# Sixteen rows of one K tile in each layer are loaded apart, in loads of eight partitions

## The chip, the cores and the metric

The kernel runs on one core of one Trainium2 chip. The metric is the device time of one execution in microseconds; several executions are timed and the median is taken. One more execution is recorded by the hardware profiler, and all rows shown come from that one.

## The reference, cut to what matters

Two layers of attention over a cache and a gated mixer, for a batch of 2 and one new token, all in bfloat16:

```python
def _A_ref(x, k_cache, v_cache, wq, wo):      # k_cache, v_cache: (2, 32, 16384, 128)
    q = (x @ wq).reshape(B, Sq, H, Dh).transpose(0, 2, 1, 3)
    scores = einsum("bhqd,bhkd->bhqk", q, k_cache) * (Dh ** -0.5)
    p = softmax(scores)
    o = einsum("bhqk,bhkd->bhqd", p, v_cache)
    return o.transpose(0, 2, 1, 3).reshape(B, Sq, H * Dh) @ wo

x = x + _A_ref(_layernorm(x), k_cache, v_cache, wq, wo)     # layer 0
x = x + _B_ref(_layernorm(x), w1, w2, w3, w4)               # a small mixer
x = x + _A_ref(_layernorm(x), k_cache, v_cache, wq, wo)     # layer 1
x = x + _B_ref(_layernorm(x), w1, w2, w3, w4)
```

Each layer reads the whole cache: 64 heads (batch times 32) with 4 MB of K and 4 MB of V each. With two layers less one pair that is kept, and the weights, 1092 MB are read.

## The kernel before

Heads are handled in pairs, 32 pairs a layer. A pair's K, and its V, is one tile of 8 MB: 128 partitions, 65536 bytes in each. Partition p holds 256 consecutive tokens of one head (64 partitions a head), so a tile is 128 rows that lie in memory one after the other.

On-chip memory has three slots for tiles. In the steady part of a layer slot A takes each pair's K and slot V each pair's V; the third is work space. `Store` (line 269) keeps a queue of planned loads (`plan`, line 278), each with a name, a semaphore, a place, a size and a list of transfers. A load is issued as soon as the cells of its place are free (`pump`, line 289), by SyncE (SP) through `Graph.dma` (line 85), which issues the listed transfers one after the other on one semaphore; its full count is 16 for each transfer, and who needs the tile waits for the full count. All data loads go through SP's one queue, in the planned order K(s), V(s-1), K(s+1), V(s) and so on (`tile_order`, line 639).

When a K tile has landed, GpSimd (POOL) passes this on to TensorE and VectorE (`landed`, line 1319; the relay is line 187 of the profile). VectorE multiplies half of the tile's blocks by q (`product`, line 1489) and sums later (`gather`, line 1501). TensorE transposes the other half (`transposed`, line 1405), ScalarE copies the transposed blocks out (`evacuate`, line 1428), and TensorE makes the scores (`scores`, line 1438). When the last block of the K tile has been read, SP issues the next K into slot A. Then comes the softmax of this pair and, when its V has landed, p times V of the pair before (`pv`, line 1567), after which SP issues the next V. Pairs 2 to 30 of layer 0 and 3 to 30 of layer 1 run in a loop.

`plan_tile` (line 488) plans a tile's load as one transfer of 128 partitions, or in column parts where `cuts` are given. `plan_all` (line 549) calls it for every tile of layer 0 (line 569) and, for layer 1, in a loop at line 593. `plan_small` (line 541) loads w2 (layer 0) and w1 (layer 1) in two transfers; the second has the last 64 rows of the weight and goes to partitions 64 to 127 alone. In layer 0 it stands in the queue right ahead of the first K tile.

Of the kernel before, what the change touches and what calls it, by code (L numbers as in the profile page):

```python
# [338 lines left out]
class KB:  # L339
# [28 lines left out]
    }  # L368
    PART = 46592
    REST = [(55808, 9728), (46592, 9216)]  # L370
    LAST_V = [(0, 32768), (32768, 16384), (49152, 16384)]
    EC = 96

# [111 lines left out]
    def slot(self, i):  # L485
        return self.AUX + self.EXTRA + i * self.TILE

    def plan_tile(self, T, t, u, slot, cuts=None):
        b, j = u % self.B, u // self.B
        src = T[b, 2 * j:2 * j + 2].rearrange("h (p j) d -> (h p) (j d)", p=self.HALF)  # L490
        if cuts is None:
            self.store.plan((t, u), f"tile{slot}", self.slot(slot), self.TILE, [(lambda m: m, src)])
            return
        have = self.parts.get((t, u), (0, []))[1]
        self.parts[t, u] = self.slot(slot), have + [lo for lo, n in cuts] + [0] * ((t, u) == self.partly())
        for lo, n in cuts:
            self.store.plan((t, u, lo), f"part{slot}_{lo // 4096}", self.slot(slot) + lo, n,
                            [(lambda m: m, src[:, lo // 2:(lo + n) // 2])])
# [50 lines left out]
    def plan_all(self):  # L549

        B, D = self.B, self.D
        row, w3r, wqr = 2 * D, 2 * self.F, 2 * 128 * self.H
        g = [row * n + CELL for n in self.GROUPS[1]]
        self.cuts, self.korder = {}, {}
        s = [self.slot(i) for i in range(self.NSLOT)]
        source = {"k": self.K, "v": self.V}

        tiles = self.tile_order(0)
        V, A, C = range(3)
        assert tiles[:2] == [("k", 0), ("k", 1)]  # L560
        assert tiles[-3:] == [("k", self.W - 1), ("v", self.W - 2), ("v", self.W - 1)]
        full = lambda k, m, at: (k, 0, m, at)
        hd, mt = self.H, self.MT
        self.store.plan(None, "xin", 0, 0, [(self.rows[0:B, :], self.A_x.rearrange("b s d -> (b s) d"))], ["prod"])
        self.plan_cols("wq", 0, self.wq, [full(k, hd, s[C] + wqr * k) for k in range(self.KT)])
        self.plan_small("w2", 0, self.w2, s[C] + wqr * (self.KT - 1) + wqr // 2, (0, 64))
        for i, (t, u) in enumerate(tiles):
            last = i == len(tiles) - 1
            self.plan_tile(source[t], t, u, C if i == 1 or last else A if t == "k" else V, self.LAST_V if last else None)
        r8 = row * self.HG  # L570
        assert r8 == w3r

        def halves(n, pieces):
            return [(k, (h or 0) * n // 2, n if h != 0 else n // 2, at) for k, h, at in pieces]
        w = self.WINDOW
        self.plan_heads(0, w["wo"], 2)
        self.plan_cols("w3", 0, self.w3, halves(mt, w["w3"]))
        self.plan_groups(0, w["w4"])
        self.plan_cols("wq", 1, self.wq, halves(hd, w["wq"]))

        tiles = self.tile_order(1)
        assert tiles[:2] == [("k", self.W - 2), ("k", 0)] and tiles[2] == self.partly()
        tiles[:3] = tiles[2], tiles[0], tiles[1]
        q = self.TILE // 4
        e = self.HOLD * self.CH * 256
        two = [(2 * q * j, 2 * q) for j in range(2)]
        self.plan_tile(source["k"], *tiles[1], A, [(0, e)])
        self.plan_tile(source["v"], *tiles[0], V, self.REST)
        self.plan_tile(source["k"], *tiles[1], A, [(e, q - e)] + [(q * j, q) for j in range(1, 4)])
        self.plan_tile(source["k"], *tiles[2], C, two)  # L590
        assert tiles[4][0] == "v" and tiles[5][0] == "k"
        for i, (t, u) in enumerate(tiles[3:]):
            self.plan_tile(source[t], t, u, C if i == len(tiles) - 4 else A if t == "k" else V, two if i in (1, 2) else None)
        assert t == "v"
        a = s[V]
        ats = []
        for _, lo, hi in self.cuts["wo", 0][-2:]:
            ats.append(row * (hi - lo))
        ats = [r8] * (self.ng - 1) + ats
        ats = [a + sum(ats[:i]) for i in range(len(ats))]  # L600
        self.plan_heads(1, ats)
        a += r8 * self.ng
        self.plan_small("w1", 1, self.w1, a, (0, 64))
        a += row * self.KT
        self.plan_cols("w3", 1, self.w3, [full(k, mt, a + w3r * k) for k in range(self.KT)])
        a += w3r * (self.KT - 1) + w3r // 2
        assert a % CELL == 0 and a + sum(g) <= self.size
        self.plan_groups(1, [a + sum(g[:i]) for i in range(len(g))], CELL)
# [1056 lines left out]
```

## Time and profile before

| | |
|---|---|
| median of 3 runs | 2545.57 us (2545.31 to 2546.1) |
| the profiled execution | 2544.21 us |
| its span on the core | 2542.5 us |
| busy: PE, VectorE, ScalarE, POOL | 56%, 70%, 44%, 1% |
| bytes read | 1092.44 MB, 430 GB/s over the span |
| loads of whole tiles, K and V | 60 and 60 |

The span is the time from the first to the last instruction of the core; the execution's own time is 1.7 us longer. The page gives the busy share of each engine in 40 slices of the span and, beside it, the mean busy share of the core's 16 DMA engines and the rate in GB/s. A table of stretches gives the same for any stretch; it books a DMA packet whole in the stretch in which it starts, so in short stretches the share can exceed 1, while GB/s divided by share remains the rate of those packets. The chain of waits goes back from the last instruction to whatever released it, step by step; a DMA in it is shown from its issue to its landing.

### The profile page before, as it was taken

To read this page: it belongs to the slowest core of one execution; us is meant where nothing else is said; L and a number is where in the kernel's file an instruction comes from. 1 tells how busy PE (TensorE), PEld (TensorE's weight loads), DVE (VectorE), ACT (ScalarE), POOL (GpSimd) and SP (SyncE) were. 2 spreads that over 40 slices of the span, in tenths; PEclk is the share of its full clock that TensorE was granted. 3 is DMA by queue.
4 is the path that set the end of the run, shared out by engine and by line. 5 is a ranking of instruction groups with operands and counts; after the bars stand their busy time and mean duration, and the time that the engine had idled before them with its cause. 6 is when DMAs were issued, how large, how long until landed. Compare 5 with 4: busy or idle time off the path is not lost.

```text
span 2542.5 us, 74290 instructions
## 1 busy us (share of the span) xinstructions
PE 1426.6 (56%) x34671; PEld 1332.8 (52%) x34671; DVE 1767.6 (70%) x1129; ACT 1126.3 (44%) x1705; POOL 29.7 (1%) x100
## 2 busy tenths in 40 slices
PE   4654654654555555546678555555465465555555
PEld 3554544554545545445567555454454455455555
DVE  4876866867767767668439777686686676776773
ACT  3453443543544534534447345345354354453451
POOL 0000000000000000000000000000000000000000
PEclk9665665666656656656656566566566666665665
DMA  9999999999999999999999999999999999999999
GB/s 415 429 434 434 434 432 435 431 434 434 435 434 429 434 435 434 431 437 433 403 411 428 436 430 436 433 434 433 433 435 431 433 434 436 432 433 435 432 431 376
DMA packets 28806, 1093.33 MB, mean 430 GB/s; under 512 B 3146, under 2 KB 4812, under 8 KB 9420
## 3 DMA queue, kind: packets, MB, share of 16 engines
q1 hardware_dynamic: 28748, 1092.45, 99.7%
q8 instruction: 49, 0.80, 0.1%
q14 instruction: 9, 0.07, 0.0%
HBM read 1092.44 MB, written 0.00 MB: 430 GB/s over the span
## 4 chain that ended last, share of the span: by engine, by line
DMA 70%; ACT 13%; PE 12%; issue 2%; DVE 2%; SPq 1%; POOLq 0%; DVEq 0%; POOL 0%
DMA mem<-in_A_v_cache_dram 35%; DMA mem<-in_A_k_cache_dram 33%; ACT mem L1430 12%; PE mps L1576 9%; PE tps L1412 2%; DMA mem<-in_B_w_dram 1%; SPq L98 1%; PE sps L1450 1%; DVE s_dve L1486 1%; DMA mem<-in_A_wo_dram 1%; ACT mem L766 0%; DVE s_dve L1507 0%; DVE prod L1482 0%; DMA mem<-in_A_wq_dram 0%; DVE mem L1497 0%
## 5 line engine op out<-in xcount | busy, mean ns | idle before, releaser
L1430 ACT ACTIVATE mem<-tps 128x1024 bf16<-128x1024 bf16 x835 | 811.4, 1093 | 535.7 <-PE tps L1412 532.5
L1507 DVE TENSOR_REDUCE s_dve<-mem 128x32 f32<-128x4096 bf16 x228 | 1007.1, 4417 | 3.9
L1412 PE MATMUL tps<-ident,mem 128*128 128x128 bf16 x6776 | 600.6, 250 | 718.1 <-POOLq L187 718.1
L1497 DVE TENSOR_TENSOR mem<-mem 128x4096 bf16<-128x4096 bf16 x228 | 507.2, 2287 | 590.9 <-POOLq L187 590.9
L1412 PEld LDWEIGHTS tps<-ident,mem 128*128 128x128 bf16 x6776 | 490.1, 114 | 723.7 <-POOLq L187 723.4
L1576 PE MATMUL mps<-p,mem 128*128 128x2 bf16 x16384 | 450.2, 165 | 94.5 <-POOLq L187 66.6
L1576 PEld LDWEIGHTS mps<-p,mem 128*128 128x128 bf16 x16384 | 443.6, 104 | 106.5 <-POOLq L187 71.7
L1450 PE MATMUL sps<-q_col,mem 128*128 128x2 bf16 x8176 | 360.4, 165 | 156.4 <-ACT mem L1430 133.3
L1450 PEld LDWEIGHTS sps<-q_col,mem 128*128 128x128 bf16 x8176 | 300.9, 98 | 222.1 <-ACT mem L1430 215.6
L1541 ACT ACTIVATE mx<-mx 128x2 f32<-128x2 f32 x64 | 13.0, 203 | 592.0 <-POOL mx L1532 591.9
L1430 ACT ACTIVATE mem<-sps 128x1024 bf16<-128x1024 bf16 x171 | 191.1, 1117 | 0.0
L1412 PE MATMUL sps<-ident,mem 128*128 128x128 bf16 x1464 | 131.9, 243 | 0.4 <-DVE prod L1074 0.4
L1412 PEld LDWEIGHTS sps<-ident,mem 128*128 128x128 bf16 x1464 | 105.1, 111 | 0.5 <-DVE prod L1074 0.5
L1486 DVE TENSOR_REDUCE s_dve<-prod 128x16 f32<-128x2048 bf16 (+1 forms) x44 | 98.5, 2238 | 1.8 <-ACT p L1545 0.4
L1365 ACT ACTIVATE mem<-sps 128x128 bf16<-128x128 f32 x63 | 17.5, 278 | 176.0 <-PE sps L1361 176.0
L1482 DVE TENSOR_TENSOR prod<-mem 128x2048 bf16<-128x2048 bf16 (+1 forms) x44 | 52.8, 1201 | 40.7 <-POOLq L187 39.1
L1361 PE MATMUL sps<-ident,q_col 128*64 128x128 bf16 x126 | 20.0, 314 | 103.0 <-DVE q_col L1348 103.0
L1361 PEld LDWEIGHTS sps<-ident,q_col 128*64 128x64 bf16 x126 | 8.3, 128 | 108.3 <-DVE q_col L1348 108.3
L1545 ACT ACTIVATE p<-s_dve,mx 64x128 bf16<-64x128 f32 (+2 forms) x126 | 54.6, 434 | 13.3 <-PE sps L1558 5.3
L1532 POOL PARTITION_ALL_REDUCE mx<-mx x64 | 25.1, 392 | 2455.4 <-DVE mx L664 2455.4
L1551 ACT ACTIVATE p<-sps,mx 64x128 bf16<-64x128 f32 (+2 forms) x128 | 51.4, 402 | 2.3
L1564 DVE COPY o_acc<-mps 128x2 f32 (+1 forms) x64 | 10.2, 160 | 41.4 <-PE mps L1576 39.5
(119 smaller groups left out, 359.3 us busy)
## 6 DMA issues: line engine op xcount, KB each, us to landing
mem<-in_A_k_cache_dram SPq DMA_DIRECT2D x4, 4096.0 KB, 16.2
mem<-in_A_v_cache_dram SPq DMA_DIRECT2D x3, 4096.0 KB, 21.4
mem<-in_A_wq_dram SPq DMA_DIRECT2D x8, 1024.0 KB, 7.8
mem<-in_B_w_dram SPq DMA_DIRECT2D x14, 576.0 KB, 7.0
mem<-in_A_k_cache_dram SPq DMA_DIRECT2D x3, 2048.0 KB, 12.1
mem<-in_B_w_dram SPq DMA_DIRECT2D x7, 864.0 KB, 21.6
mem<-in_B_w_dram SPq DMA_DIRECT2D x4, 1152.0 KB, 19.2
mem<-in_A_v_cache_dram SPq DMA_DIRECT2D x2, 2048.0 KB, 48.0
```

The lines of the kernel that those rows point to most:

```text
L98: sp.dma_start(dst, src).then_inc(h, 16)
L1361: ins = pe.matmul(qps[e * h:(e + 1) * h, :], lhsT=q, rhs=self.ident[:, :], start=True, stop=True, skip_group_check=True)
L1412: ins = pe.transpose(out[:, j * 128:(j + 1) * 128], buf[:, j * 128:(j + 1) * 128], self.ident[:, :])
L1430: self.act(lambda e: e.activation(out=self.kt[k], in_=src.rearrange("p (i c) -> p i c", i=self.CH), func=ACT.Copy), reads=bk, writes=self. ...
L1450: ins = pe.matmul(self.sps[sp][:, b:b + 2], lhsT=kt[:, j, :], rhs=self.q_col[:, 2 * sp:2 * sp + 2], start=True, stop=True, skip_group_chec ...
L1482: self.dv(lambda e: e.tensor_tensor(out=prod, in0=buf.rearrange("p (j d) -> p j d", d=128), in1=qbc, op=ALU.mult), reads=self.spilt(("qb", ...
L1486: self.dv(lambda e: e.tensor_reduce(out=sd[:, c0:c0 + DB], in_=prod, axis=AX.X, op=ALU.add), reads=["prod"], writes=self.spilt(("s_dve", m ...
L1497: self.dv(lambda e: e.tensor_tensor(out=prod, in0=buf.rearrange("p (j d) -> p j d", d=128), in1=qbc, op=ALU.mult), reads=self.spilt(("qb", ...
L1507: self.dv(lambda e: e.tensor_reduce(out=sd[:, c0:c0 + n], in_=prod, axis=AX.X, op=ALU.add), reads=pk, writes=self.spilt(("s_dve", m)), to= ...
L1545: self.act(lambda e, i=i, at=at: e.activation(out=two(self.p[at, :, i])[:, :, pb:], in_=two(self.s_dve[m][at, 0:self.NB - n]), func=ACT.Ex ...
L1551: self.act(lambda e, i=i, at=at: e.activation(out=two(self.p[at, :, i])[:, :, 0:pb], in_=two(self.sps[m][at, i:2 * n:2]), func=ACT.Exp, bi ...
L1576: ins = pe.matmul(self.mps[:, 448:450], lhsT=buf[:, j * 128:(j + 1) * 128], rhs=self.p[:, b0 + j, :], start=b0 + j == 0, stop=b0 + j == se ...
```

## The change

For two tiles, K of pair 16 in layer 0 and K of pair 16 in layer 1, `plan_tile` lists several transfers in place of one. `UNEVEN` gives for each a number of bytes `at`, 18432 and 0. Partitions 0 to 111 are loaded whole in one transfer. Of partitions 112 to 127, the first `at` bytes of each row are loaded in one transfer of 16 partitions (left out where `at` is 0), and the rest in two transfers, of partitions 112 to 119 and 120 to 127. So layer 0's tile has four transfers and layer 1's three. The bytes, their places, the semaphore of the slot and all instructions of the other engines stay the same; the count that is waited for grows with the number of transfers. The tiles with `cuts` are not touched.

```diff
+    UNEVEN = {(0, "k", 16): 18432, (1, "k", 16): 0}
...
-    def plan_tile(self, T, t, u, slot, cuts=None):
+    def uneven(self, src, at):
+
+        n, a = self.TILE // 2, at // 2
+        rows = [(0, 112, 0, n)] + [(112, 128, 0, a)] * (a > 0) + [(112, 120, a, n), (120, 128, a, n)]
+        return [(lambda m, p=p, q=q, x=x, y=y: m[p:q, x:y], src[p:q, x:y]) for p, q, x, y in rows]
+
+    def plan_tile(self, T, t, u, slot, cuts=None, l=None):
         b, j = u % self.B, u // self.B
         src = T[b, 2 * j:2 * j + 2].rearrange("h (p j) d -> (h p) (j d)", p=self.HALF)
         if cuts is None:
-            self.store.plan((t, u), f"tile{slot}", self.slot(slot), self.TILE, [(lambda m: m, src)])
+            at = self.UNEVEN.get((l, t, u))
+            all_ = [(lambda m: m, src)] if at is None else self.uneven(src, at)
+            self.store.plan((t, u), f"tile{slot}", self.slot(slot), self.TILE, all_)
             return
...
-            self.plan_tile(source[t], t, u, C if i == 1 or last else A if t == "k" else V, self.LAST_V if last else None)
+            self.plan_tile(source[t], t, u, C if i == 1 or last else A if t == "k" else V, self.LAST_V if last else None, 0)
...
-            self.plan_tile(source[t], t, u, C if i == len(tiles) - 4 else A if t == "k" else V, two if i in (1, 2) else None)
+            self.plan_tile(source[t], t, u, C if i == len(tiles) - 4 else A if t == "k" else V, two if i in (1, 2) else None, 1)
```

## The prediction

> **What bounds the kernel now.** I read the slices and the queues on the page first, then the chain of waits, then a table of stretches at the places where the DMA engines differ from each other.
>
> ```profile
> span 2542.5 us, 74290 instructions
> PE 1426.6 (56%) x34671; PEld 1332.8 (52%) x34671; DVE 1767.6 (70%) x1129; ACT 1126.3 (44%) x1705; POOL 29.7 (1%) x100
> ...
> DMA  9999999999999999999999999999999999999999
> GB/s 415 429 434 434 434 432 435 431 434 434 435 434 429 434 435 434 431 437 433 403 411 428 436 430 436 433 434 433 433 435 431 433 434 436 432 433 435 432 431 376
> ...
> q1 hardware_dynamic: 28748, 1092.45, 99.7%
> q8 instruction: 49, 0.80, 0.1%
> ...
> DMA 70%; ACT 13%; PE 12%; issue 2%; DVE 2%; SPq 1%; POOLq 0%; DVEq 0%; POOL 0%
> ```
>
> No compute engine is above 70%, and the data queue's packets fill 99.7% of sixteen engines' span. In the steady slices the rate is 434 GB/s, 27.1 GB/s an engine. A K or V tile is 128 rows of 65536 bytes, eight rows an engine, so one row costs 65536 / 27.1 GB/s = 2.42 us and a tile 19.35 us. A pair (K and V) should take 38.7 us, and the chain at the place of the change shows just that:
>
> ```profile
> 612.87 25.99 DMA mem<-in_A_k_cache_dram
> 638.87 0.02 issue
> ...
> 638.96 1.05 PE tps L1412 x8
> 640.01 0.02 issue
> 640.03 11.11 ACT mem L1430 x12
> 651.14 0.05 issue
> 651.19 0.37 PE sps L1450 x8
> 651.56 0.02 issue
> 651.57 26.00 DMA mem<-in_A_k_cache_dram
> ```
>
> One K is issued at 612.87 and the next at 651.57, 38.70 us later. The next K is issued 12.7 us after the K before it has landed on its last engine (638.87). So every microsecond by which the slowest engine delivers a K later delays the next issue, and as the engines are full, nothing later gives it back.
>
> The engines are not level. The last loads' engines run dry in this table (columns: stretch, its length, busy time and count of PE, weight loads, DVE, ACT and POOL, clock, DMA share, GB/s):
>
> ```profile
> 2534.50:2535.00 0.50, 0.32 (x12) 0.23 (x9) 0.00 (x0) 0.00 (x0) 0.00 (x0) 0.50 0.93 369
> 2535.00:2535.50 0.50, 0.38 (x10) 0.37 (x11) 0.00 (x0) 0.00 (x0) 0.00 (x0) 0.50 0.70 281
> 2535.50:2536.00 0.50, 0.50 (x19) 0.49 (x19) 0.05 (x1) 0.25 (x2) 0.00 (x0) 0.50 0.53 219
> 2536.00:2536.50 0.50, 0.50 (x25) 0.50 (x23) 0.30 (x2) 0.50 (x1) 0.00 (x0) 0.50 0.50 207
> 2536.50:2537.00 0.50, 0.24 (x10) 0.15 (x6) 0.00 (x0) 0.50 (x1) 0.00 (x0) 0.50 0.49 198
> 2537.00:2537.50 0.50, 0.01 (x1) 0.01 (x1) 0.02 (x1) 0.44 (x2) 0.00 (x0) 0.50 0.50 196
> 2537.50:2538.00 0.50, 0.50 (x19) 0.50 (x20) 0.15 (x1) 0.00 (x0) 0.00 (x0) 0.50 0.52 187
> 2538.00:2538.50 0.50, 0.50 (x24) 0.50 (x20) 0.00 (x0) 0.00 (x0) 0.00 (x0) 0.50 0.32 122
> 2538.50:2539.00 0.50, 0.50 (x21) 0.47 (x19) 0.00 (x0) 0.00 (x0) 0.00 (x0) 0.50 0.26 95
> ```
>
> From 2535.5 to 2538.0 the share stands at one half: eight engines have finished all their work and eight have not, though all had the same data. The 49 instruction packets, each of 16 KB on one engine, are the likeliest cause in the list; nothing else there is dealt unevenly. The chain's last DMA ends at 2539.24:
>
> ```profile
> 2515.22 24.01 DMA mem<-in_B_w_dram
> ```
>
> Adding up the idle shares (0.07, 0.30, 0.47, 0.50, 0.51, 0.50, 0.48, 0.68, 0.74, and 0.24 us after 2539.0) gives 2.4 us: that is all that a perfect levelling could bring at this end.
>
> **The change part by part.** In layer 1, sixteen rows of one K (1 MB) leave the load that is dealt over sixteen engines and go out as two loads of eight rows. That a load of few rows uses as few engines shows at the input, a load of two rows:
>
> ```profile
> 1.72:1.77 0.05, 0.00 (x0) 0.00 (x0) 0.00 (x0) 0.05 (x1) 0.00 (x0) 1.00 0.14 43
> ```
>
> A share of 0.14 is 2.2 of sixteen engines: two packets. So I take eight engines for eight rows, the same eight both times. They get 7 + 2 = 9 rows, the others 7 instead of 8: +2.42 and -2.42 us of work. In layer 0 the first 18432 bytes of the sixteen rows stay spread over all engines and 47104 bytes move: +-1.74 us. [...] No row here shows engine numbers.
>
> The issues. Two more in layer 1, three more in layer 0:
>
> ```profile
> L98 SPq DMA_DIRECT2D mem<-in_A_k_cache_dram x69: 327/328/636, 4.9 to 2435.3; - x69
> 2486.44 0.43 SPq L98
> ...
> 612.87 0.33 SPq L98 DMA_DIRECT2D mem<-in_A_k_cache_dram  x1
> 626.66 0.33 SPq L98 DMA_DIRECT2D mem<-in_A_v_cache_dram  x1
> ```
>
> At 0.43 us for an issue right behind another that is 0.9 and 1.3 us on SP's queue, where the next thing is a V issue 13.8 us later: hidden, and without that cover 2.2 us at most. No wait is added. POOL still waits once for the whole tile, for a larger count, and behind its relays stand the transposes on PE, the products on DVE and, through the buffer, SP's next K. They all wait for the last of the small loads.
>
> The rate of the small loads is the dear question. The nearest row is the one load here that fills half the partitions: 64 rows of 1152 bytes at the end of w2, four an engine, with the first K right behind it. This table takes packets in the stretch in which they start, so GB/s divided by the DMA share is the rate of those packets while they ran:
>
> ```profile
> 15.74:16.06 0.32, 0.32 (x18) 0.32 (x16) 0.00 (x0) 0.00 (x0) 0.00 (x0) 1.00 8.19 3262
> 35.30:35.60 0.30, 0.00 (x0) 0.00 (x0) 0.00 (x0) 0.00 (x0) 0.00 (x0) 1.00 7.09 3059
> 54.65:55.00 0.35, 0.35 (x8) 0.24 (x5) 0.35 (x1) 0.35 (x2) 0.00 (x0) 1.00 4.34 1873
> ```
>
> The first rows of the first K, behind that load, ran at 3262 / 8.19 = 398 GB/s; those of the next two tiles at 431 and 432. That is 2.63 instead of 2.43 us, +0.20 us on each engine. The four small rows take 4 x 1152 / 27.1 GB/s = 0.17 us, so a load to half the partitions that ran at half the rate would leave just such a backlog.
>
> So I read it that fewer partitions can be filled only at a lower total rate. Bounds for eight rows: at best no loss, 2.42 us a load; at worst in proportion to the partitions, 434 / 16 = 27.1 GB/s for 524288 bytes, 19.35 us, a factor of 8. I take a factor of 4, 9.7 us, near the middle (4.5): the half-partition row speaks for a full loss, but rows that lie close together may share a way while others do not, which no row here shows. [...]
>
> The sum, on the eight engines that get the small loads:
> - layer 1: two loads at 9.7 us in place of one row of 2.42: +16.9 us (bounds +2.4 and +36.3);
> - layer 0: 18432 bytes to sixteen partitions, 0.68 us at full rate, by the same factor 2.7, then two loads of 47104 bytes, 6.95 each, less 2.42: +14.2 us (bounds +1.7 and +30.8);
> - the 112-row loads: seven rows, 16.9 us, but to 7/8 of the partitions, so up to 19.35: +2.4 us a layer, +4.8 (bounds 0 and +4.8);
> - the lead that the levelling takes off: the spread of the two halves covers part of it. The early half has some time to spare before it costs anything: I take the gain of the levelled case below, -1.2 us in layer 1 and, as no view shows layer 0's end as cleanly, -1.3 there: -2.5 (bounds -4.8 and 0).
>
> That is 16.9 + 14.2 + 4.8 - 2.5 = +33.4 us. The profiled execution took 2544.21 us, 1.7 more than its span, and the median of the runs is 2545.57, 1.36 above it. I put the sum on the median: 2579.0 us.
>
> **The rivals.**
> Levelled, no loss: the small loads run at full rate and go to the early half. For it: the clean split into halves, and that only eight engines are touched. Then the early half ends 2.42 us later in layer 1, about 2538.0 instead of 2535.6, and the late half 2.42 earlier, so the end moves from 2539.24 to about 2538.0: -1.2 us. For layer 0 with its 1.74 us I take about the same, -1.3. Time 2543.1. Its ceiling is 2 x 2.4 = 4.8 us, short of 0.2% (5.1 us, about what a measurement of this kernel can tell from no change). It decides if the factor on small loads is below about 1.3: (1.3 - 1) x 4.84 us = 1.5 us eats the gain. Against it: the 398 GB/s.
> Wrong half: full rate, but the small loads fall to the late engines. +2.42 + 1.74 = +4.2 us, 2549.8. No view names engines, so I can't exclude it.
> Nothing moves: the eight-row loads are dealt over all sixteen engines after all. Then only the issues are added, hidden: 2545.6. Against it: the two-row load on two engines.
>
> **How the numbers follow.** Slow small loads 0.58, with a range of its own of 2560 to 2612 (bounds of the terms); levelled 0.27; wrong half 0.10; nothing moves 0.05. Faster by over 0.2% needs more than the ceiling: 0.03, out of levelled. Slower: 0.58 and 0.03 of the wrong half. The rest, 0.36, is no change. The range from 2542 to 2605 takes in the rivals and leaves out the dearest end.
>
> **What the profile would show.** If I am right, in the chain the K issued near 613 lands some 40 us after its issue instead of 26, the next K issue follows about 14 us late, a stretch of some 15 us behind the 112 rows has a DMA share well under 1, and the like happens around pair 16 of layer 1, after which the 38.7 us rhythm is back. If the levelling is all, those rows stay at 26 us, and the step at one half near the end of the table shrinks. It would be wrong if the 0.20 us behind the 64-row load is due to something else than its partitions, such as where its rows lie in memory.

## The result: 2.8% slower, twice the forecast loss

| | before | after |
|---|---|---|
| median of 5 runs each | 2545.54 us | 2614.99 us (2612.92 to 2618.44) |
| ratio after to before | | 1.0277, 95% interval 1.0265 to 1.0288 |
| span of the profiled execution | 2542.5 us | 2613.3 us |

The change costs 69.5 us; 33.4 us were forecast. The page after, its slices and queues:

```profile
span 2613.3 us, 74295 instructions
...
DMA  9999999999999999999999999999999999999999
GB/s 416 426 433 433 434 432 433 433 433 318 352 425 437 432 434 434 433 433 433 395 415 426 437 434 432 433 434 434 433 434 210 410 431 429 432 431 431 432 434 375
...
q1 hardware_dynamic: 28812, 1092.45, 99.5%
```

The bytes are the same and the engines are as busy as before (99.5%, no slice below 9 tenths). What fell is the rate: to 318 and 352 GB/s in the slices around pair 16 of layer 0, to 210 in that of layer 1. So this is hardly idle time. SyncE's issues (start, time spent issuing, count) show that it stays in those two places:

```profile
613.38 1.50 SPq L98 DMA_DIRECT2D mem<-in_A_k_cache_dram  x4
...
683.78 0.35 SPq L98 DMA_DIRECT2D mem<-in_A_k_cache_dram  x1
...
722.21 0.33 SPq L98 DMA_DIRECT2D mem<-in_A_k_cache_dram  x1
...
1963.80 1.04 SPq L98 DMA_DIRECT2D mem<-in_A_k_cache_dram  x3
...
2041.26 0.35 SPq L98 DMA_DIRECT2D mem<-in_A_k_cache_dram  x1
...
2079.63 0.33 SPq L98 DMA_DIRECT2D mem<-in_A_k_cache_dram  x1
```

From the issue of the changed K to the next K issue it is 683.78 - 613.38 = 70.4 us in layer 0 and 77.5 us in layer 1, instead of 38.7: +31.7 and +38.8 us, 70.5 together. The next distances are 38.4 us in both layers, so the rhythm is back at once. This distance is the yardstick of all that follows. The chain after shows the landing (it can't name the queue of a tile with several loads):

```profile
631.84 39.24 another core or an unknown queue
671.08 0.02 issue
...
683.78 25.72 DMA mem<-in_A_k_cache_dram
```

K lands at 671.08, 57.7 us after its issue instead of 26, and the next issue still follows 12.7 us later. How the rate goes through layer 1's tile, in stretches of 5 us (last three columns: clock, DMA share, GB/s):

```profile
1960.00:1965.00 5.00, 4.09 (x99) 3.74 (x96) 4.96 (x4) 5.00 (x7) 0.00 (x0) 1.00 1.04 446
1965.00:1970.00 5.00, 1.38 (x26) 0.93 (x26) 5.00 (x3) 2.31 (x4) 0.00 (x0) 0.74 1.01 249
1970.00:1975.00 5.00, 1.36 (x51) 1.36 (x52) 4.96 (x2) 0.00 (x0) 0.00 (x0) 0.50 0.97 210
1975.00:1980.00 5.00, 5.00 (x194) 5.00 (x191) 3.27 (x2) 0.00 (x0) 0.00 (x0) 0.50 0.96 210
...
1985.00:1990.00 5.00, 0.00 (x0) 0.00 (x0) 0.00 (x0) 0.00 (x0) 0.00 (x0) 0.50 1.37 354
1990.00:1995.00 5.00, 0.00 (x0) 0.00 (x0) 0.00 (x0) 0.00 (x0) 0.00 (x0) 0.50 0.99 210
1995.00:2000.00 5.00, 0.00 (x0) 0.00 (x0) 0.00 (x0) 0.00 (x0) 0.00 (x0) 0.50 1.48 210
2000.00:2005.00 5.00, 0.00 (x0) 0.00 (x0) 0.00 (x0) 0.00 (x0) 0.00 (x0) 0.50 1.06 105
2005.00:2010.00 5.00, 0.00 (x0) 0.00 (x0) 0.00 (x0) 0.00 (x0) 0.00 (x0) 0.50 0.98 105
2010.00:2015.00 5.00, 0.00 (x0) 0.00 (x0) 0.00 (x0) 0.00 (x0) 0.00 (x0) 0.50 0.78 92
2015.00:2020.00 5.00, 0.00 (x0) 0.00 (x0) 0.00 (x0) 0.00 (x0) 0.00 (x0) 0.50 0.73 118
2020.00:2025.00 5.00, 0.00 (x0) 0.00 (x0) 0.00 (x0) 0.00 (x0) 0.00 (x0) 0.50 0.61 184
...
2035.00:2040.00 5.00, 4.71 (x104) 4.12 (x102) 5.00 (x4) 5.00 (x7) 0.00 (x0) 1.00 0.70 301
2040.00:2045.00 5.00, 2.61 (x56) 2.01 (x56) 4.96 (x2) 4.49 (x5) 0.00 (x0) 0.75 0.71 262
```

Two levels stand out. From 1970 on, while the 112 rows are loaded, all engines are busy at half the rate: 210 / 0.97 / 16 = 13.5 GB/s an engine, 4.84 us a row (the stretch from 1985 is somewhat faster, 354 / 1.37 / 16 = 16.1 GB/s). From 2000 to 2010, in the eights, the share is still about 1 and the rate a quarter: 105 / 0.98 / 16 = 6.7 GB/s, 9.8 us a row. The eights are taken to be on eight engines only, which no row names but the times fit: alone, below, the two take 19.7 us, where all sixteen rows in one load take 11.8. If so, the other eight engines, which are already at V's rows, are slowed as well; of the 34 rows that start between 1998 and 2016, 9.4 us each in the mean (stretches of 1 us, added up), at most sixteen are in eights. I had forecast the second level for eight engines alone and not the first.

### The profile page after: what moved, and what is told of

It is laid out like the page before. It is cut to its first block, busy times and chain, and to the rows that moved or that the text cites. A ratio compares the mean times of both kernels' runs of the same rounds, so it can differ in the third digit from the quotient of the medians.

```text
span 2613.3 us, 74295 instructions
## 1 busy us (share of the span) xinstructions
PE 1428.0 (55%) x34671; PEld 1337.3 (51%) x34671; DVE 1767.1 (68%) x1129; ACT 1126.7 (43%) x1705; POOL 29.6 (1%) x100
## 3 DMA queue, kind: packets, MB, share of 16 engines
q1 hardware_dynamic: 28812, 1092.45, 99.5%
## 4 chain that ended last, share of the span: by engine, by line
DMA 68%; PE 16%; ACT 7%; another core or an unknown queue 4%; issue 3%; SPq 1%; DVE 1%; POOLq 0%; POOL 0%; DVEq 0%
DMA mem<-in_A_v_cache_dram 49%; DMA mem<-in_A_k_cache_dram 17%; PE mps L1585 13%; ACT mem L1439 6%; PE tps L1421 2%; DMA mem<-in_B_w_dram 1%; SPq L98 1%; PE sps L1459 0%; ACT mem L775 0%; DVE s_dve L1516 0%; DMA mem<-in_A_wq_dram 0%; DVE mem L1506 0%; PE sps L1421 0%; PE sps L936 0%
## 5 line engine op out<-in xcount | busy, mean ns | idle before, releaser
L1573 DVE COPY o_acc<-mps 128x2 f32 (+1 forms) x64 | 10.2, 159 | 46.8 <-PE mps L1585 45.0
```

## The experiments

The theory ("ways"): a load's rate depends on which partitions its engines write at the same time, as if neighbours shared a way into the on-chip memory. What such a way is, and how many there are, no row shows; the runs can only show which partitions are slow together. Rivals: the number of transfers, the uneven count of rows ("balance"), and where the rows lie in HBM ("memory"). In all kernels below `uneven` takes a list of loads, each given by its partitions (first, end, step), its columns in bytes and, where they differ from the partitions, the rows of the tile in memory:

```diff
+    def uneven(self, src, parts):
+        out = []
+        for rows, *rest in parts:
+            x, y, *frm = rest or (0, self.TILE)
+            d, s = slice(*rows), slice(*(frm[0] if frm else rows))
+            out.append((lambda m, d=d, x=x, y=y: m[d, x // 2:y // 2], src[s, x // 2:y // 2]))
+        return out
```

### As many loads, cut by columns

```diff
+    UNEVEN = {
+        (0, "k", 16): [((0, 128), x, y) for x, y in ((0, 18432), (18432, 32768), (32768, 49152), (49152, 65536))],
+        (1, "k", 16): [((0, 128), x, y) for x, y in ((0, 24576), (24576, 45056), (45056, 65536))]}
```

> The tiles of the change are cut by columns instead of partitions: four loads of 128 partitions in layer 0, three in layer 1. Theory 'ways' (engines that write into neighbouring partitions share a way, so the loss is in which partitions one load writes): nothing changes, 2545.6 us, within 5 us. Rival 'transfers' (each added load costs: 70 us for five added ones, 14 us each): about 2615 us.

Measured: 2545.49 us against 2545.09, ratio 1.0001 (0.9991 to 1.0010). The added issues and the larger count cost nothing; the rival "transfers" is out.

### Without the eights

```diff
+    UNEVEN = {(l, "k", 16): [((0, 112),), ((112, 128),)] for l in (0, 1)}
```

> In both layers the tile is 112 partitions and then 16 partitions, whole; no loads of eight. Ways: seven rows at the 4.8 us each that the changed kernel's trace shows (33.6 us) and a row of sixteen neighbours at 4.8 to 9.7 us, 38.4 to 43.3 us in place of 19.35: +19 to +24 us a layer, 2584 to 2594 us. Rival 'balance' (all loss comes from nine rows on eight engines and seven on the others): every engine has eight rows again, 2545.6 us. My own recorded terms: +2.4 us a layer for the 112 rows and +2.4 to +7.3 us for the sixteen, 2555 to 2565 us.

Measured, in one run: 2597.34 us, +52, with distances of 67.4 and 64.6 us. Every engine has eight rows here, if 112 and 16 rows are dealt evenly, so balance is out too, and three quarters of the loss need no load of eight. The ways had 2594 at most; the sum was a little short.

### Nine ways to load a K tile

```diff
+    UNEVEN = {(l, "k", u): rows for l in (0, 1) for u, rows in {
+        4: [((0, 128), 0, 32768), ((0, 128), 32768, 65536)],
+        7: [((0, 112),)],
+        10: [((16, 128),)],
+        13: [((0, 112),), ((112, 128),)],
+        16: [((0, 112),), ((112, 120),), ((120, 128),)],
+        19: [((0, 112),), ((112, 128, 2),), ((113, 128, 2),)],
+        22: [((0, 64),), ((64, 128),)],
+        25: [((0, 96),), ((96, 128),)],
+        28: [((0, 120),), ((120, 128),)]}.items()}
```

> Nine K tiles in each layer are loaded in nine ways (pairs 4, 7, 10 to 28), and each is read from the distance between its K issue and the next, 38.7 us where nothing is changed. Pairs 7 and 10 leave out sixteen of the partitions. By ways: pair 4, two halves by columns, 38.7 us; pair 7, partitions 0 to 111 alone, 38.7 + 33.6 - 19.35 = 53 us; pair 10, 16 to 127 alone, 53 us; pair 13, 112 and 16, 58 to 63 us; pair 16, the change as in layer 1, 77 us; pair 19, as 16 but the eights with every second partition, so twice the ways, 68 us; pair 22, two loads of 64, half rate, 58 us; pair 25, 96 and 32, 58 us; pair 28, 120 and 8, over 58 us. Rival 'balance': 38.7 us where all engines have eight rows (4, 13, 22, 25), 36.3 us for seven (7, 10), 41.1 us for nine (28), and 19 as 16. Rival 'memory' (it is where the rows lie in HBM): 10 differs from 7, and 19 from 16 by chance only.

| pair | loads | distance, layer 0 and 1, us |
|---|---|---|
| 4 | two halves by columns | 38.8, 38.8 |
| 7 | 0 to 111 alone | 55.2, 53.5 |
| 10 | 16 to 127 alone | 55.1, 57.2 |
| 13 | 112 and 16 | 64.5, 68.6 |
| 16 | the change as in layer 1 | 77.0, 77.2 |
| 19 | the eights on every second partition | 69.2, 68.9 |
| 22 | 64 and 64 | 65.6, 66.3 |
| 25 | 96 and 32 | 60.0, 62.3 |
| 28 | 120 and 8 | 75.6, 76.3 |

The row of pair 7 in layer 1, issues again:

```profile
1798.79 0.33 SPq L98 DMA_DIRECT2D mem<-in_A_k_cache_dram  x1
...
1852.25 0.33 SPq L98 DMA_DIRECT2D mem<-in_A_k_cache_dram  x1
```

One load of 112 partitions, with an eighth less to move than the whole tile, takes 15 us longer than it. That is most of the missing loss, and it stands at both places where the 112 partitions begin (0 and 16). Pair 19 is 8 us shorter than 16, as the ways say (69 against 68 expected). Pair 22 was expected at 58 and came to 66: two loads of 64 neighbours cost another 8 us beyond half rate.

### Eights of a quarter of the columns

```diff
+    UNEVEN = {(l, "k", u): rows for l in (0, 1) for u, rows in {
+        4: [((0, 128), 0, 49152)] + [((8 * i, 8 * i + 8), 49152, 65536) for i in range(16)],
+        8: [((0, 128), 0, 49152)] + [((i, 128, 16), 49152, 65536) for i in range(16)],
+        12: [((0, 128), 0, 49152)] + [((32 * j + i, 32 * j + 32, 4), 49152, 65536) for j in range(4) for i in range(4)],
+        16: [((0, 128), 0, 49152)] + [((8 * i, 8 * i + 8), 49152, 65536, (i, 128, 16)) for i in range(16)],
+        20: [((0, 128), 0, 49152)] + [((i, 128, 16), 49152, 65536, (8 * i, 8 * i + 8)) for i in range(16)],
+        24: [((i, 128, 8),) for i in range(8)],
+        28: [((i, 128, 2),) for i in range(2)]}.items()}
```

> Seven K tiles in each layer: three quarters of the columns as one load of 128 partitions, and the last quarter as sixteen loads of eight rows of 16384 bytes (0.605 us each at 27.1 GB/s, 9.7 us on eight engines instead of 4.84). Read from the distance to the next K issue. By ways: pair 4, eight neighbouring partitions, a quarter of the rate, 38.7 us for the sixteen loads, 72.6 us; pair 8, every sixteenth partition, half the rate, 53 us; pair 12, every fourth of 32 partitions, full rate, 43.5 us; pair 16, eight neighbouring partitions filled with every sixteenth row of the memory (the tile's rows change places), 72.6 us as pair 4; pair 20, every sixteenth partition filled with eight neighbouring rows of the memory, 53 us as pair 8; pair 24, the whole tile in eight loads of every eighth partition, half the rate, 58 us; pair 28, in two loads of every second partition, 38.7 to 58 us. Rival 'memory': pair 16 goes with pair 8 and pair 20 with pair 4. Rival 'balance': all of 4 to 20 at 43.5 us, 24 and 28 at 38.7 us.

Measured (layer 0, layer 1): pair 4 57.8, 56.6; pair 8 59.8, 57.4; pair 12 52.4, 51.6; pair 16 57.4, 56.4; pair 20 60.5, 57.0; pair 24 63.8, 65.5; pair 28 38.7, 38.8. Here the ways missed: neighbours (4) should have cost some 20 us more than every sixteenth partition (8) and cost a little less. No run had shown the half rate expected for every sixteenth partition or the full rate for every fourth; why pairs 4 and 8 are alike is not shown. The exchange of rows (16 against 4, 20 against 8) changed nothing, which speaks against memory but little, as 4 and 8 are alike. The clear rows are pair 28, two loads of every second partition with no loss at all where 64 neighbours cost 27 us, and pair 12. There the first eight short loads go to partitions 0 to 63 and the last eight to 64 to 127 (stretches of layer 1):

```profile
1952.00:1956.00 4.00, 0.00 (x0) 0.00 (x0) 0.00 (x0) 1.03 (x6) 0.00 (x0) 0.50 0.94 401
1956.00:1960.00 4.00, 0.00 (x0) 0.00 (x0) 0.00 (x0) 0.00 (x0) 0.00 (x0) 0.50 1.06 311
1960.00:1964.00 4.00, 0.00 (x0) 0.00 (x0) 0.00 (x0) 0.00 (x0) 0.00 (x0) 0.50 1.10 229
```

GB/s by share falls from 427 to 293 to 208: from full rate to half, on busy engines, as the loads come to the upper partitions and V's rows run beside them. Why the short loads to the upper partitions go with the drop and those to the lower ones do not is not shown; the trace has no engine numbers.

### Memory against partitions

```diff
+    UNEVEN = {(l, "k", u): rows for l in (0, 1) for u, rows in {
+        4: [((0, 64), 0, 65536, (0, 128, 2)), ((64, 128), 0, 65536, (1, 128, 2))],
+        7: [((0, 128, 2), 0, 65536, (0, 64)), ((1, 128, 2), 0, 65536, (64, 128))],
+        10: [((0, 112),)],
+        13: [((32 * i, 32 * i + 32),) for i in range(4)],
+        16: [((i, 128, 4),) for i in range(4)],
+        19: [((16 * i, 16 * i + 16),) for i in range(8)],
+        22: [((0, 112),), ((112, 128, 2), 0, 65536, (112, 120)), ((113, 128, 2), 0, 65536, (120, 128))],
+        25: [((0, 112),), ((112, 120), 0, 65536, (112, 128, 2)), ((120, 128), 0, 65536, (113, 128, 2))],
+        28: [((0, 112, 2),), ((1, 112, 2),)]}.items()}
```

> Nine more ways of loading a K tile, in both layers, read from the distance to the next K issue (38.7 us undisturbed). In pairs 4, 7, 22 and 25 the rows of the memory and the partitions are matched another way, so some of the tile's rows change places; pairs 10 and 28 leave out sixteen partitions. Ways (the partitions decide): pair 4, two loads of 64 neighbouring partitions filled with every second row of the memory, 66 to 68 us as seen for 64 neighbours before; pair 7, every second partition filled with 64 neighbouring rows, 38.7 us; pair 10, partitions 0 to 111 alone again, 53 to 55 us; pair 13, four loads of 32 neighbours, 66 to 97 us; pair 16, four loads of every fourth partition, 38.7 us if their engines are dealt ways of their own as with every second, else 58 to 68 us; pair 19, eight loads of 16 neighbours, 97 us at a quarter of the rate, 66 us if one load overlaps the next; pair 22, the eights on every second partition filled with neighbouring rows, 69 us; pair 25, the eights on neighbouring partitions filled with every second row, 77 us; pair 28, partitions 0 to 111 as two loads of every second partition (56 rows, fourteen engines), 38.7 us if they get ways of their own, 54 us or more if not. Rival 'memory' (the rows' places in HBM decide): pair 4 38.7 us, pair 7 66 to 68 us, pair 22 77 us, pair 25 69 us.

```profile
148.51 1.12 SPq L98 DMA_DIRECT2D mem<-in_A_k_cache_dram  x2
...
211.35 0.33 SPq L98 DMA_DIRECT2D mem<-in_A_k_cache_dram  x1
...
288.65 1.14 SPq L98 DMA_DIRECT2D mem<-in_A_k_cache_dram  x2
...
327.36 0.33 SPq L98 DMA_DIRECT2D mem<-in_A_k_cache_dram  x1
```

Pair 4, neighbouring partitions with rows apart in memory: 62.8 us (62.5 in layer 1). Pair 7, partitions apart with neighbouring rows: 38.7 (38.7). The partitions decide; "memory" is out, but for some 3.5 us between 62.6 and the 66 us of pair 22 above. The rest, layer 0 and 1: pair 10 55.3, 51.8; pair 13 67.1, 63.6; pair 16 38.7, 38.7; pair 19 96.3, 90.0; pair 22 69.9, 61.6; pair 25 77.2, 73.9; pair 28 63.7, 62.6. The two layers of a pair differ by up to 8 us (pair 22), so smaller differences between pairs say little. The rates within loads of 64, 32 and 16 neighbours (pairs 4, 13 and 19, layer 0):

```profile
165.00:185.00 20.00, 0.86 (x33) 0.78 (x30) 0.87 (x4) 2.09 (x9) 0.36 (x1) 0.50 0.98 203
560.00:580.00 20.00, 0.00 (x0) 0.00 (x0) 0.00 (x0) 2.10 (x9) 0.27 (x1) 0.50 1.01 206
850.00:870.00 20.00, 0.00 (x0) 0.00 (x0) 0.00 (x0) 0.00 (x0) 0.00 (x0) 0.50 0.91 105
```

64 and 32 neighbours have the same rate, 203 and 206 GB/s, near half, and 16 a quarter, 105. So the rate is not in proportion to the partitions. Nor does a load have to cover each partition to be fast: loads of every second and of every fourth partition ran without loss in pairs 7 and 16 (38.7 us).

### Each kind of load alone

```diff
+    UNEVEN = {(l, "k", u): rows for l in (0, 1) for u, rows in {
+        4: [((112, 120),), ((120, 128),)],
+        8: [((112, 128, 2),), ((113, 128, 2),)],
+        12: [((112, 128),)],
+        16: [((112, 128), 0, 18432), ((112, 120), 18432, 65536), ((120, 128), 18432, 65536)],
+        20: [((0, 112), 0, 65536, (0, 224, 2))],
+        24: [((0, 112),)],
+        28: [((0, 64),)]}.items()}
...
-        src = T[b, 2 * j:2 * j + 2].rearrange("h (p j) d -> (h p) (j d)", p=self.HALF)
+        src = T[b, 2 * j:2 * j + (4 if (t, u) == ("k", 20) else 2)].rearrange("h (p j) d -> (h p) (j d)", p=self.HALF)
```

The rest of each of these tiles is left out; for pair 20 the source is widened to two pairs' K, of which every second row is taken.

> Seven K tiles in each layer are loaded only in part, so that each kind of load is seen without the others; the rest of those tiles isn't loaded. Before, a K lands 26 us after its issue, 6.6 us for what is ahead of it and 19.35 for itself, and the next K issue comes 12.7 us later; so the distance to the next K issue is 19.3 us plus what the loads take. Ways: pair 4, the two eights of layer 1 alone, 2 x 9.7 us, 38.7 us; pair 8, the same on every second partition, 9.7 us, 29 us; pair 12, partitions 112 to 127 in one load, 9.7 us, 29 us; pair 16, layer 0's three small loads, 2.7 + 2 x 6.95, 35.9 us; pair 20, partitions 0 to 111 filled with every second row of two pairs' K, 54 us as with neighbouring rows; pair 24, partitions 0 to 111, 52 to 55 us; pair 28, partitions 0 to 63 alone, four rows at 5.1 us, 40 us. Rival 'the 112 rows slow what follows' (the eights are cheap by themselves and dear only behind the 112 rows): pair 4 24 us, pairs 8, 12 and 16 22 to 24 us. Rival 'memory': pair 20 differs from pair 24 by more than the 3.5 us by which pair 24's like differed so far. At full rate pair 28 would be 29 us.

```profile
148.61 0.63 SPq L98 DMA_DIRECT2D mem<-in_A_k_cache_dram  x2
...
186.47 0.35 SPq L98 DMA_DIRECT2D mem<-in_A_k_cache_dram  x1
...
302.59 1.41 SPq L98 DMA_DIRECT2D mem<-in_A_k_cache_dram  x2
...
332.85 0.33 SPq L98 DMA_DIRECT2D mem<-in_A_k_cache_dram  x1
```

The two eights alone: 37.9 us (40.2 in layer 1), 38.7 expected. On every second partition: 30.3 (29.7), 29 expected; that nearly halves their time, to 10.7 us from 19.7. Sixteen neighbours: 31.3 (30.9), 29 expected. Layer 0's three small loads: 36.9 (36.4), 35.9 expected. So the eights are dear by themselves and as dear as forecast; the rival "the 112 rows slow what follows" is out. The 112 rows filled from rows apart in memory: 50.8 (51.1), against 52.5 (55.6) from neighbouring rows: memory is at most some 4 us of their loss, not the 15, and perhaps less, as the loads from neighbouring rows spread from 51.8 to 55.6 us by themselves. Partitions 0 to 63 alone: 43.9 (46.9), 40 expected.

### The same surplus in loads four partitions apart

```diff
+    UNEVEN = {(l, "k", 16): [((0, 128), 0, 57344)] + [((32 * j + i, 32 * j + 32, 4), 57344, 65536)
+                                                     for j in range(4) for i in range(4)] for l in (0, 1)}
```

> The same surplus of one row of 65536 bytes on eight engines, in both layers, without a load of 112 partitions and without neighbouring eights: seven eighths of the columns of all 128 partitions, then the last 8192 bytes in sixteen loads of eight partitions, four apart. Rival 'levelled' of the prediction (uneven numbers of rows help when no load is slow): 2543.1 us. Rival 'balance' (the surplus of 2.42 us on eight engines costs what it is): 2550.4 us. Ways: the eight loads to partitions 0 to 63 run at full rate, 0.30 us each, those to 64 to 127 at half, 0.60 us, as the same loads of 16384 bytes did, 7.3 us in place of 2.4, and what shares the ways is slowed too: scaled from the 13 us that the wider ones cost, about 6.6 us a layer, 2558.7 us.

Measured: 2558.88 us against 2544.74, ratio 1.0055 (1.0038 to 1.0071), as the ways had it (2558.7, scaled from the wider short loads of pair 12 above). The distance in layer 0, and the rate beside the upper short loads:

```profile
613.00 11.08 SPq L98 DMA_DIRECT2D mem<-in_A_k_cache_dram  x17
...
659.83 0.33 SPq L98 DMA_DIRECT2D mem<-in_A_k_cache_dram  x1
...
638.00:642.00 4.00, 0.00 (x0) 0.00 (x0) 0.00 (x0) 0.00 (x0) 0.00 (x0) 0.50 1.04 244
```

46.8 us, 46.2 in layer 1. The surplus brings no gain here, but this run is not free of slow loads: from 638 to 642 the engines move 244 / 1.04 = 235 GB/s, little over half. So it does not show what a surplus at full rate would do.

### The change's split on partitions that lie apart

```diff
+    UNEVEN = {
+        (0, "k", 16): [((0, 128, 4),), ((1, 128, 4),), ((2, 128, 4),), ((3, 128, 8),), ((7, 128, 8),)],
+        (1, "k", 16): [((0, 128, 4),), ((1, 128, 4),), ((2, 128, 4),), ((3, 128, 8),), ((7, 64, 8),), ((71, 128, 8),)]}
```

> The change's own split, seven rows on every engine and the other sixteen apart, but with partitions that lie apart: the 112 rows are three loads of every fourth partition (32 each) and one of every eighth (16). In layer 1 the other sixteen rows are two loads of eight, every eighth partition of one half each, in layer 0 one load of sixteen. Ways (only the choice of partitions matters): six rows at 2.42 us and one at 5.1, 19.6 us for the 112, then 4.8 us for each eight or 5.1 for the sixteen: layer 0 24.7 us in place of 19.35, distance to the next K issue 44 us (67 with 112 and 16 neighbours); layer 1 29.3 us, distance 49 to 52 us (77 in the change), the upper end if the eights slow the V rows beside them; 2561 to 2565 us in all. Rival 'seven rows' (112 rows dealt seven to an engine are slow wherever they go): layer 0 about 62 us, layer 1 about 65 us, some 2595 us. Rival 'balance': 38.7 and 41.1 us, 2548 us.

```profile
613.25 3.04 SPq L98 DMA_DIRECT2D mem<-in_A_k_cache_dram  x5
...
660.39 0.33 SPq L98 DMA_DIRECT2D mem<-in_A_k_cache_dram  x1
...
1940.13 3.71 SPq L98 DMA_DIRECT2D mem<-in_A_k_cache_dram  x6
...
1994.45 0.33 SPq L98 DMA_DIRECT2D mem<-in_A_k_cache_dram  x1
```

Measured, in one run: 2567.88 us (2561 to 2565 expected); 47.1 us in layer 0 (44 expected, 67 with 112 and 16 neighbours) and 54.3 in layer 1 (49 to 52 expected, 77 in the change). If rows are dealt evenly, the engines in layer 1 have as many rows as in the change, and the choice of partitions takes 23 of its 39 us away. Layer 0 has no eights; against 112 and 16 neighbours, it takes 20 of 29 us away. So seven rows to an engine are not slow in themselves.

## Why the prediction was wrong

**The sign and what carries it were right.** The loss sits in the two K tiles, the next K issue waits for the last small load, the rhythm is back after one pair, and the issues are hidden (by the four and three column loads, 2545.49 us). The 0.20 us behind the 64-row load fits its partitions: 64 neighbours run near half rate (203 GB/s) from neighbouring rows of the memory and from rows apart (66 and 62.6 us).

**The small loads were sized right.** Two eights at 9.7 us, 19.4: alone they took 39.0 - 19.35 = 19.7 us (mean of both layers; 19.35 is the part of the distance that isn't the tile's own load). Layer 0's three, 2.7 + 2 x 6.95 = 16.6: alone 36.7 - 19.35 = 17.3 us. So the factor of 4 held. By the rows of this case it was a choice near the middle between 1 and 8, so that it came out so well is partly luck. That both eights go to the same eight engines, as the sum has it, no run shows; the 19.7 us, twice 9.8, are what a row of each on the same engines would take at the rate seen from 2005 to 2010 (9.8 us a row).

**The step that failed is the 112-row loads.** I put seven rows at 16.9 us and took 7/8 of the partitions for at most 19.35, +2.4 us a layer with bounds of 0 and +2.4. Six such loads alone gave distances of 51.8 to 55.6 us, 54.0 in the mean: 34.6 us for the load, 17.7 over 16.9. That is 15.3 us a layer more than forecast, 30.6 of the 36.1 us that were missing. The fault was to read the 64-row load as "rate in proportion to partitions" and to go from half to seven eighths in a straight line, while for the eights I allowed that rows close together share a way. In these runs there is a step between 128 partitions (434 GB/s) and fewer neighbours (203 to 210 with 32 to 120), not a slope. Within a load of 64 neighbours alone, and within one of 120 (pair 28 of the nine ways), the rate is the same 210 GB/s as with 112:

```profile
1095.00:1100.00 5.00, 4.75 (x178) 4.75 (x179) 4.01 (x2) 0.00 (x0) 0.00 (x0) 0.50 1.02 210
...
1278.00:1283.00 5.00, 0.00 (x0) 0.00 (x0) 0.00 (x0) 0.00 (x0) 0.00 (x0) 0.50 1.02 210
```

**The range.** It left out the dearest end by choice. The prediction's 2560 to 2612 are not the bounds of its terms: these add up to -0.7 and +71.9 us, 2544.9 to 2617.5. The measured 2614.99 lies inside that, but by another road: the bounds allow for small loads twice as dear as they were, and for 4.8 us of the 112-row loads, which cost 35.4 (17.7 a layer).

**The levelling gain did not show.** With a gain, the step at one half would have shrunk. The end of the changed kernel:

```profile
2605.50:2606.00 0.50, 0.13 (x5) 0.04 (x2) 0.00 (x0) 0.00 (x0) 0.00 (x0) 0.50 0.83 327
2606.00:2606.50 0.50, 0.29 (x8) 0.28 (x9) 0.00 (x0) 0.00 (x0) 0.00 (x0) 0.50 0.58 230
2606.50:2607.00 0.50, 0.50 (x19) 0.48 (x17) 0.00 (x0) 0.19 (x1) 0.00 (x0) 0.50 0.50 194
2607.00:2607.50 0.50, 0.50 (x24) 0.50 (x22) 0.35 (x2) 0.48 (x2) 0.00 (x0) 0.50 0.48 162
2607.50:2608.00 0.50, 0.33 (x13) 0.24 (x10) 0.00 (x0) 0.50 (x1) 0.00 (x0) 0.50 0.24 94
```

The shares after it are 0.18, 0.13, 0.09 and 0.06, up to the last DMA's end at 2610.02. The idle shares add up to 3.0 us instead of 2.4, and to 2.7 in the run cut by columns, in which every load keeps its 128 partitions. So nothing supports the -2.5 us; the levelled run, 14 us slower than before, can't give the sign of the term by itself, as it has slow loads too. Why there is no gain is not shown.

**Put together** from the parts measured alone: layer 1 34.6 + 19.7 - 19.35 = +34.9 us, measured +38.8; layer 0 34.6 + 17.3 - 19.35 = +32.6, measured +31.7. Of 70.5 us the parts make 67.5; the rest lies in how the loads overlap each other and V. The 15 us with a share "well under 1" did not come as idle time. The shares of 0.61 to 0.78 from 2010 to 2025 are booked so because packets count where they start: the eight stretches from 1985 to 2025 have shares that add up to 8.0. V's rows beside the eights were slowed and kept their engines busy. Engines ran dry only around the late K issue, at shares of 0.70 and 0.71 from 2035 to 2045, some 3 us.

**Open:** which engine takes which of the 112 rows. The trace names neither engine nor partition of a packet. So that 112 neighbours reach half of the rate is measured (210 against 434 GB/s), and why just half is not shown. Nor is it shown why every second of 112 partitions loses (63.7 us) and every second of 128 does not (38.7 us).

## What to carry to other kernels

Keep loads at all 128 partitions and cut them by columns, which cost nothing here (2545.49 us against 2545.09). Where a load can't have them all, take every second or every fourth of the whole 128 rather than neighbours: at the same bytes two loads of 64 neighbours came to 62.6 and 66 us, near half the rate (203 GB/s), and two of 64 alternate partitions to the 38.7 us of the whole tile. Alternate partitions of only 112 are no help (63.7 and 62.6 us). When the busy share of the DMA engines stays at 1, read the GB/s beside it: here busy engines were at a quarter of their speed (105 GB/s at a share of 0.98), in the eights and in V's rows beside them.

## What the runs showed of the hardware that I had not expected

- A load of 112 neighbouring partitions runs at 210 GB/s, half of the 434 of one with 128; it takes 34.6 us where the whole tile, with more bytes, takes 19.35.
- Every second and every fourth of 128 partitions: no loss (38.7 us). Every eighth: 63.8 and 65.5 us, near half rate. Every second of 112 (56 rows): 63.7 and 62.6 us, no better than neighbours.
- Slow loads slow the next tile: the 34 rows that start from 1998 to 2016 took 9.4 us each in the mean in place of 2.42, and at most sixteen of them are in eights; the others, V's by their order, ran at a quarter too (105 GB/s at a share of 0.98).
- Where rows lie in memory counts little: 62.6 instead of 66 us for two loads of 64 neighbours, and for 112 neighbours 50.8 and 51.1 us against 51.8 to 55.6, which is hardly beyond the spread.
